# Attention, expert attention and gated FFN in one kernel: six plain pairs instead of two, weight conversions in other places, a first load in two column halves

## The chip, the cores and the metric

The kernel runs on one core of one Trainium2 chip, in one launch. The metric is the device time of an execution in microseconds (us), median of several runs. Before the change it is 498.16 us (three runs, 498.07 to 498.64). PE is the matmul engine, DVE, ACT and POOL are the vector, scalar and GpSimd engines, and SP issues DMAs. Each engine works through its own instructions in order and waits for others by semaphores.

## The reference

Four batches, 448 positions, 12 heads of 64. The output of causal attention is the input of four expert attentions, and theirs that of a gated FFN.

```python
# 1: q, k, v of (4, 12, 448, 64)
scores = scale * q @ k.T;  masked above the diagonal
attn = exp(scores - rowmax);  attn /= sum + 1e-9;  x = attn @ v     # (4, 448, 768)
# 2: four experts of width 64, the two best of x @ w_gate per position
q, k, v = x @ wq[e], x @ wk[e], x @ wv[e]
ye = causal_softmax(scale * q @ k.T) @ v @ wo[e]
out += mask * w * ye
# 3: w_in (768, 1024), w_out (1024, 768), a convolution of 3 along positions
h = relu(x @ w_in)
y = (h * sigmoid(conv3(h))) @ w_out
```

The inputs q, k, v and the expert weights come in float32, the FFN's weights in float64.

## The kernel before

Everything is a task of a small planner (`Program`, with `add` for each task): an engine, an assumed cost, what it needs, and which ring buffer or PSUM bank it takes or frees. Tasks are put out in the order of a table, ORDER, which `steps_of` decodes into pairs of task and engine. It fixes the order of every engine's instructions, and for a task made with `either` also the engine. Where the planner's costs leave PE idle for over 0.7 us, it puts dummy matmuls of an identity (L1563) in between.

Precision is kept by splitting a float32 number into a high part of fewer bits and a low part, its remainder, and by adding products of those parts. The attention works on pairs of heads (A, batch, pair 0 to 5):

- A **split pair** loads q and k of each head twice over the partitions (`nat`, L543), makes high parts (L350, L352 or L356) and two low parts (L359), and multiplies stacked 128 rows in one pass per block (L665). Each head takes one of the three `skA` buffers.
- A **plain pair** loads q and k of both heads once (`load_plain`, L556) into one buffer and multiplies them as plain float32, each head in its half of the 128 rows (`pair_scores`, L622). Before, pairs 0 and 1 of batch 0 are plain.

A head has four blocks of 112 rows, of 112 to 448 columns. Behind the scores come DVE's masked row maxima (L678), ACT's exponentials with their sums (L687), the normalisation on ACT or POOL (L350, L352), transposes on PE (L718), copies out of PSUM (PT), the product with v (L789), and the split of the transposed output xT (L821).

Beside batch 0's attentions the weights are prepared. `fold_piece` multiplies w_in into the experts' wo: twelve pieces of 512 columns, each loaded as float64 (`wraw`, L891), made into float32 by an ACT square (L443) and four DVE steps (L448, L452, L456, L460), split into high (ACT, L898) and low (POOL, L901), and multiplied by 12 matmuls (L910). `proj_weights` loads the experts' q, k, v and gate weights in six slices (`praw`, 512 and 260 columns) and splits them: high on ACT (L954), low on DVE (L958). `wraw` and `praw` share a ring of two buffers. The projections (L981, L1027), the FFN (L1323) and its output products (L1456) follow. The expert pairs of a batch run among the next batch's attentions.

The first load is pair 0 of batch 0: one head on SP's queue, the other on ACT's (L561). SP then loads wo, pair 1 and the first split heads.

Of the kernel before, what the change touches and what calls it, by code (L numbers as in the profile page):

```python
# [17 lines left out]
ALU = mybir.AluOpType  # L18
# [16 lines left out]
    "H>iFzNV?6?qK#-Wfk7A~q%sF_W4I2y1s^2z;Dw}<%(t0WnfIAQJeMFQToFLx3-mmC8T}jacVa(&4ZVdPL<5-<=rqBCcA<CC7D6{+j4+5F#iQ_l"
    "pfAvA^c3L^jRw?20w5$_XHxMN(gFIGASFG+KgTcPm+;f*b^IRw5dVqznYc~bC4E4DPku(G0$jihSO9=XAkGt32~-l5=mM@tO2R1`O@@IqDFh&Z"
    "p16sBPIyh&CL9q?2_oPrFbYfovw)WrA}s*N1cdaQ{F0m?C&^M`2k;0uAX$m{Oj@QC*dYv(`ba-8zY?D_Uow}01Sv@ZC|Bg~vih=yveW>coFaFV"
    "&IoC;i?|9zGZXj|{2BfsX`D0w%#q#!?}15D5;y}cfm_m#WCA5c;!x7SJSj%>5?4s8q}R+-<_(idIb+hu9P%4Lf{|i~EH#G4GGHDOH^^_u5#k=u"
    "OB^On6YrQ-%szRXq9rd<Zpl*eEr7x3$)m(RqJTV0bYX<7pO|l$`^>k@Z!z7NevE)3qYPox6gS00@nRyFG0ZmQn6gV*rc6;Tn6I*=EH(?pQnL&!"
    "8`(#WlZlv4vWt8|IiM_Mtz|6|b!-#c&zizav+S%D)+~#P;b7KScD9@CWCh8+WG`igVxfd7U6h|No0wh9D&>rFh`FSYvM^bnDaV*4VvrT1^pS_i"  # L40
    "d#poNk`>3S5x>dl$mz-Hru>?9l696fKpCXOSskna_6qx!(#z^&4YNjBNz5*Lh&|1oWv{X6S)wdWmLcnL&PvW+&S}mJ<|SqY^N##|)@0UfR*IFv"
    "NV7OuwyaN>8%%&5VLxCW=B(wsXKk|1a^_i=tTanmtE&B#dCS7*pmL}=V2(V;P;0Gq)uwZP&f3XR<-oNM*%}VSIm~*R<I1|oxy7Kd#+=QZIH#Wj"
    "XANWzXOCx3XU}DCXTzKz$H3|2jMeUCFJ`Z0FJ(t-W3`>NqihRjkn=0|gnN{o$Ue<J&%Vq~XZO_h*ACTA<UGrHo)gcV&K=0@%q7=7tG&+#s6;BA"
    "3Q}LxzO3D^U9J^T)l?bvFK#zylRd^U*KO4PTszM`V873q;uxtmDn#{B!_+u+Hutc0o-?1@L7nCFP|vuRTr7CZ?x)`7bmyXThjNqb6nivxggQ#S"
    "WnX38WF6No=l)hJ%(-A&bAGSg;C!mR&w56EP6e{%*_v!(wlSNYovyvB#n!R2h1t|PPMs|q%JyXkvytr8+^yVivp=%|4xJ<7;5jd;uc;f<Evm2%"
    "4=!<ba|yYrTsB9_d7mq*Q`dFYS?a!UF}znfP|iN}EmfS`Q}?9qnEH`=MrDB8oFmSA&M9Z4PLaFAA@MXcBh5yGXg->&4z3H;A$2e7#_FEcQFGb3"
    "np|71K6jY5P8*{w*KO48*L|YCtvku}<py(|xo4ak>OB>p9pql+-sf)7c4&vR_q0hGoD<4Hv$^0LZGpB#`;Prxwvq0mTj@^vb?%G05Isgu(#~j~"
    "X&CyCE+YF2?Gp{;33(6?=1F-(nucfKy|4RN*G2E4579^Iee@~%Ed4cogZ_pd<Xv&DIS8+Vx9YO+5<Gx^#iOx_bSj;|2k8QOl9%Ff_yRti2GY{J"
    "JC2;LqEq=V>3j48dJnIkcgqvdB;ao@1*irS^dubu2f#Q8gF$czoC0NhHUFG`NuL2Hc}~8JHVSrv-Jq8bvW09J+XMn!0{0dFId6mqay48RcL7`m"
# [1578 lines left out]
```

## Time and profile before

| what | value |
|---|---|
| median of three runs | 498.16 us |
| profiled execution, its own time | 498.41 us |
| its span in the trace | 496.6 us |
| PE busy | 477.4 us (96%) |
| DVE, ACT, POOL busy | 414.4, 360.2, 322.7 us |
| DMA | 97.17 MB, mean 196 GB/s |

Times in the profile are of one execution, and the span begins and ends inside the time measured from outside. Matmuls are pipelined, so PE's busy time contains waiting of one for another. The chain of waits is followed back from the last instruction, and the stretches give each engine's busy time in a piece of the span.

### The profile page before, as it was taken

Reading aid. Unit: us, or ns where it says so; the run is one execution under the profiler, and the core shown is the slowest. Engines: PE = TensorE matmul, PEld = TensorE weight load, DVE = VectorE, ACT = ScalarE, POOL = GpSimd, SP = SyncE. Lnnn points to the kernel's source line nnn. Section 1 sums busy time; section 2 is a strip of 40 time slices with the busy share of each in tenths; the row PEclk is TensorE's granted clock in tenths of the full one; section 3 lists DMA queues with packets and bytes.
Section 4 is the critical chain, followed back from the end, with each engine's and each line's share of the span. In section 5 each row is a group of like instructions: output and inputs, shape, how many; then the busy total and the mean of one; then the engine's idle time right before and its main releaser. Section 6 shows DMA issues by size and latency. Waiting matters only on the chain.

```text
span 496.6 us, 10098 instructions
## 1 busy us (share of the span) xinstructions
PE 477.4 (96%) x3142; PEld 405.5 (82%) x3142; DVE 414.4 (83%) x1183; ACT 360.2 (73%) x996; POOL 322.7 (65%) x441
## 2 busy tenths in 40 slices
...
DVE  3999999998899988988889997178898997877852
...
GB/s 183 224 236 239 221 183 181 215 241 228 173 212 238 158 224 203 135 159 261 201 169 209 166 106 232 222 164 196 262 230 229 302 207 252 191 237 130 38 74 94
DMA packets 46534, 97.17 MB, mean 196 GB/s; under 512 B 5136, under 2 KB 26896, under 8 KB 46480
## 3 DMA queue, kind: packets, MB, share of 16 engines
...
HBM read 62.56 MB, written 25.69 MB: 178 GB/s over the span
## 4 chain that ended last, share of the span: by engine, by line
PE 67%; ACT 13%; DVE 9%; POOL 4%; issue 3%; DMA 3%; SPq 0%; POOLq 0%; DVEq 0%; ACTq 0%
PE bank L1456 21%; PE bank L789 10%; PE bank L665 8%; PE bank L981 8%; PE bank L1323 7%; PE bank L718 7%; ACT P_A L687 5%; PE bank L1027 4%; DVE P_A L678 2%; ACT PT_A L350 2%; ACT P_A L350 2%; DMA wraw<-in_w_in_dram 1%; POOL sk_A L359 1%; DMA wset<-wohl 1%; PE bank L1563 1%
## 5 line engine op out<-in xcount | busy, mean ns | idle before, releaser
L687 ACT ACTIVATE P_A<-P_A,nm_A 112x448 f32<-112x448 f32 (+3 forms) x192 | 99.7, 525 | 9.8 <-DVE nm_A L678 8.9
L359 POOL TENSOR_TENSOR sk_A<-nat,sk_A 64x448 fp32r<-64x448 f32 (+1 forms) x76 | 90.4, 1190 | 15.2 <-ACT sk_A L350 7.7
L678 DVE CUSTOM_DVE_ANT_0 P_A<-bank,mask 112x448 f32<-112x448 f32 (+3 forms) x192 | 79.9, 440 | 12.7 <-PE bank L622 6.9
L665 PE MATMUL bank<-sk_A 128*112 128x336 f32 (+3 forms) x352 | 65.0, 310 | 4.8 <-DVE nm_A L678 2.8
L981 PE MATMUL bank<-xT,wqk 128*128 128x448 f32 x288 | 67.8, 372 | 0.0
L718 PE MATMUL bank<-ident,P_A 112*112 112x112 f32 x480 | 59.8, 261 | 5.3 <-ACT PT_A L350 2.9
L665 PEld LDWEIGHTS bank<-sk_A 128*112 128x112 f32 x352 | 48.7, 175 | 13.8 <-DVE nm_A L678 5.7
L718 PEld LDWEIGHTS bank<-ident,P_A 112*112 112x112 f32 x480 | 48.6, 133 | 10.1 <-ACT PT_A L350 3.4
L981 PEld LDWEIGHTS bank<-xT,wqk 128*128 128x128 f32 x288 | 51.5, 188 | 3.7
L350 ACT ACTIVATE P_A<-P_A,r_A 112x336 f32<-112x336 f32 (+3 forms) x101 | 50.6, 530 | 4.6 <-DVE r_A L698 4.6
L352 POOL TENSOR_SCALAR P_A<-P_A,r_A 112x448 f32<-112x448 f32 (+3 forms) x83 | 43.5, 534 | 16.0 <-DVE r_A L698 6.8
L1456 PE MATMUL bank<-up,ws 128*128 128x448 f32 x225 | 52.8, 366 | 0.0
L789 PE MATMUL bank<-PT_A,v 112*64 112x448 f32 (+3 forms) x384 | 49.9, 405 | 1.1 <-DVE PT_A L356 1.1
L1344 DVE SCALAR_TENSOR_TENSOR bank<-h,cw,bank 128x448 f32<-128x448 f32 x64 | 43.1, 685 | 7.7 <-ACT bank L1342 4.7
L350 ACT ACTIVATE PT_A<-bank 112x336 f32<-112x336 f32 (+1 forms) x94 | 42.7, 477 | 4.2 <-PE bank L718 4.1
L789 PEld LDWEIGHTS bank<-PT_A,v 112*64 112x64 f32 x384 | 25.4, 136 | 24.9 <-issue 12.1
L1456 PEld LDWEIGHTS bank<-up,ws 128*128 128x128 f32 x225 | 42.2, 188 | 3.8
L1456 PE MATMUL bank<-us,ws 128*128 128x448 f32 x180 | 43.8, 367 | 0.0
L1027 PE MATMUL bank<-wvg,xT 128*112 128x260 f32 x288 | 42.0, 288 | 0.2 <-DVE lg L1047 0.2
L352 POOL TENSOR_SCALAR P_M<-P_M,r_M,g_w 112x224 f32<-112x224 f32 (+3 forms) x54 | 32.0, 601 | 10.0 <-DVE r_M L698 5.1
L352 POOL TENSOR_SCALAR sk_A<-nat 128x896 fp32r<-128x896 f32 x30 | 28.7, 956 | 14.3 <-DMA nat<-in_qk_dram 13.7
L687 ACT ACTIVATION_READ_ACCUMULATOR P_A<-P_A,nm_A 112x1 f32 x192 | 37.6, 196 | 0.0
...
## 6 DMA issues: line engine op xcount, KB each, us to landing
nat<-in_qk_dram SPq DMA_DIRECT2D x88, 224.0 KB, 4.3
...
g<-g SPq DMA_DIRECT2D x32, 224.0 KB, 2.5
...
v<-in_v_dram SPq DMA_DIRECT2D x24, 224.0 KB, 4.7
out_dram<-osb_c SPq DMA_DIRECT2D x24, 224.0 KB, 2.0
```

The lines of the kernel that those rows point to most:

```text
L350: nc.scalar.activation(dst, src, AF.Copy, scale=scale)
L352: nc.gpsimd.tensor_scalar(dst, src, scale, 1.0 if scale2 is None else scale2, ALU.mult, ALU.mult)
L359: (nc.gpsimd if e == "POOL" else nc.vector).tensor_tensor(dst, a, b, op)
L665: nc.tensor.matmul(sp[:CP], t[:, j.o[h], m * CP : (m + 1) * CP], t[:, j.o[h] + k, :w], start=(k == 2), stop=(k == 1),)
L678: nc.vector.tensor_tensor_reduce(rows(i), st["s", i][:CP, :w], mask[:, S - w :], -SCALE, 3.0e38, ALU.add, ALU.min, st["nm"][:, i : i + 1],)
L687: nc.scalar.activation(rows(i), rows(i), AF.Exp, bias=st["nm"][:, i : i + 1], scale=-1.0, accum_out=st["sm"][:, i, 0:1],)
L718: nc.tensor.transpose(pt[:CP, o : o + CP], rows(i)[:, kt * CP : (kt + 1) * CP], ident[:CP, :CP])
L789: nc.tensor.matmul(st["ov"][h * D : (h + 1) * D, kt * CP : S], j.v[:, kt, h, :], j.PT[h][:, col_base[kt] : col_base[kt] + S - kt * CP], st ...
L981: nc.tensor.matmul(st["ps"][:, :S], proj["wqk"][:, a, cc, w, p * P : (p + 1) * P], xT[b, cc][:, b2, :], start=(cc == 0 and (a, b2) == PASS ...
L1027: nc.tensor.matmul(st[i][:CP, :VW], xT[b, cc][:, a, i * CP : (i + 1) * CP], proj["wvg"][:, b2, cc, :], start=(cc == 0 and (a, b2) == PASSE ...
L1344: nc.vector.scalar_tensor_tensor(y, h, w, y, ALU.mult, ALU.add)
L1456: nc.tensor.matmul(ps(pb)[:, :S], wset[s][:, a, m, c2 * P : (c2 + 1) * P], unit(operands[q, c2, name][0])[:, b2], start=(c2 == 0 and (a, b ...
```

## The change

- All six pairs of batch 0 are plain (`j.p < 6`).
- The first load is cut by columns: both heads' positions 0 to 223 on SP's queue (`load_left`), positions 224 to 447 on ACT's (`load_right`), and the first pair's score blocks go from the narrowest up, the two lower ones needing the left half alone.
- The high parts of the fold's pieces may be made on ACT, DVE or POOL, the low parts on POOL or DVE; the projection weights' high parts on ACT or POOL, their low parts on DVE or POOL; the high parts of the experts' q and k on ACT or DVE.
- Two planner costs change, and the table ORDER is another.

```diff
--- before.py
+++ after.py
@@ -27,75 +27,74 @@
 
 ENGINES = ("ACT", "DVE", "PE", "POOL", "SP", "")
 ORDER = (
-    "c-jTQX-HcMfB@j+CDELkQ<IlObE&!1Txu>..."
...
+    "c-jTQ2}s)uU@-8U=GI(lE;W~$OHKZXF_-4..."
...
 )
 
 
@@ -480,7 +479,7 @@
         order += [A[b, p] for p in range(4)] + [M[b - 1, 0], A[b, 4], A[b, 5], M[b - 1, 1]]
     order += [M[B - 1, p] for p in range(NEP)]
     for j in order:
-        j.plain = j.kind == "A" and j.b == 0 and j.p < 2
+        j.plain = j.kind == "A" and j.b == 0 and j.p < 6
         j.phase = j.b if j.kind == "A" else B + j.b
 
     xT = {}
@@ -556,17 +555,24 @@
         def load_plain():
             alloc_head(j, 0)
             j.qk = f(j.sk[0][:, 0:2, :])
-            if j is order[0]:
-                for h in range(2):
-                    (nc.sync if h else nc.scalar).dma_start(j.qk[h * D : (h + 1) * D], qk[j.b, j.p, h * D : (h + 1) * D])
-            else:
-                nc.sync.dma_start(j.qk, qk[j.b, j.p])
+            nc.sync.dma_start(j.qk, qk[j.b, j.p])
+
+        def load_left():
+            alloc_head(j, 0)
+            j.qk = f(j.sk[0][:, 0:2, :])
+            nc.sync.dma_start(j.qk[:, :, : S // 2], qk[j.b, j.p, :, :, : S // 2])
+
+        def load_right():
+            nc.scalar.dma_start(j.qk[:, :, S // 2 :], qk[j.b, j.p, :, :, S // 2 :])
 
         def load_v():
             j.v = pools["head"].tile([CP, NQ, 2, D], F32, tag="vn", name=f"v_{n}", bufs=RINGS["vn"])
             nc.sync.dma_start(j.v, v[j.b, j.p])
 
-        if j.plain:
+        if j is order[0]:
+            t = add("SP", 700 + dma(224), load_left, take=[j.skb[0]], lag=LAND - 300)
+            j.ready = [t, add("SP", dma(224), load_right, [t], lag=LAND)]
+        elif j.plain:
             t = add("SP", dma(448), load_plain, take=[j.skb[0]], lag=LAND)
             j.ready = [t, t]
         else:
@@ -611,11 +617,13 @@
 
         j.scored = {}
 
+        turns = range(NQ) if j is order[0] else range(NQ - 1, -1, -1)
+
         def score(i):
             def go():
                 w = CP * (i + 1)
                 for h in (1, 0):
-                    if i == NQ - 1:
+                    if i == turns[0]:
                         head_tiles(j, h)
                     j.st[h]["s", i] = sp = ps(j.st[h]["sb", i])
                     r = slice(h * D, (h + 1) * D)
@@ -626,21 +634,21 @@
             return go
 
         first = []
-        for i in range(NQ - 1, -1, -1):
+        for i in turns:
             take = []
             for h in (1, 0):
-                if i == NQ - 1:
+                if i == turns[0]:
                     j.st[h]["Pb"] = Buf("P")
                     take.append(j.st[h]["Pb"])
                 j.st[h]["sb", i] = Buf("s")
                 take.append(j.st[h]["sb", i])
             t = add(
-                "PE", 2 * (CP * (i + 1) / 1.2 + 95), score(i), [j.ready[0]] + first,
+                "PE", 2 * (CP * (i + 1) / 1.2 + 95), score(i), [j.ready[i * 2 // NQ]] + first,
                 take=take, free=[j.skb[0]], mode=2,
             )
             first = [t]
             j.scored[i] = t
-        j.taken = [j.scored[NQ - 1]]
+        j.taken = [j.scored[turns[0]]]
         j.began += j.taken
 
     def head(j, h, moe):
@@ -893,12 +901,12 @@
         t = add("SP", dma(512), load, wo_loads, take=[raw], lag=LAND)
         t, w, buf = from_f64(lambda: st["raw"], raw, t, [P, 2, FW], n)
 
-        def hi():
+        def hi(e):
             st["whl"] = pools["stage"].tile([P, 2, 2, FW], F32R, tag="whl", name=f"whl_{qt}_{c}", bufs=RINGS["whl"])
-            nc.scalar.activation(st["whl"][:, 0], w(), AF.Copy)
-
-        def lo():
-            nc.gpsimd.tensor_tensor(st["whl"][:, 1], w(), f(st["whl"][:, 0]), ALU.subtract)
+            copy(e, st["whl"][:, 0], w())
+
+        def lo(e):
+            two(e, st["whl"][:, 1], w(), f(st["whl"][:, 0]), ALU.subtract)
 
         def prod():
             if c == 0:
@@ -915,9 +923,9 @@
                             stop=(ec == NEP - 1 and cc == NCC - 1 and (a, b2) == PASSES[2]),
                         )
 
-        th = add("ACT", act_sb(n), hi, [t], take=[whl], free=[buf])
-        tl = add("POOL", pool_tt(n), lo, [th], free=[buf])
-        t = add("PE", mm(FW, 4 * NEP * 3 // 2) + 104, prod, [th, tl] + wo_done + last, take=[mb] if c == 0 else [], free=[whl])
+        th = add(either("fhi", 0, of_one(n)), 0, hi, [t], take=[whl], free=[buf])
+        tl = add(either("fol", 0, of_two(n)), 0, lo, [th], free=[buf])
+        t = add("PE", mm(FW, 4 * NEP * 3 // 2) + 30, prod, [th, tl] + wo_done + last, take=[mb] if c == 0 else [], free=[whl])
         fold_tasks.append(t)
         return [t]
 
@@ -949,18 +957,20 @@
                     (proj["wvg"][:, :, cc], r[:, 2 * ED :]),
                 )
 
-            def hi(cc=cc, st=st):
+            def hi(e, cc=cc, st=st):
                 for d, s in parts(cc, st):
-                    nc.scalar.activation(d[:, 0], s, AF.Copy)
-
-            def lo(cc=cc, st=st):
+                    copy(e, d[:, 0], s)
+
+            def lo(e, cc=cc, st=st):
                 for d, s in parts(cc, st):
-                    nc.vector.tensor_tensor(d[:, 1], s, f(d[:, 0]), ALU.subtract)
+                    two(e, d[:, 1], s, f(d[:, 0]), ALU.subtract)
 
             n = 2 * ED + VW
             t = add("SP", dma(386), load, take=[raw], lag=LAND)
-            th = add("ACT", 94 + act_sb(n), hi, [t], free=[raw])
-            tl = add("DVE", 60 + dve(n), lo, [th], free=[raw], port=True)
+            eng = either("phi", 0, {"ACT": 94 + act_sb(n), "POOL": 161 + pool_ts(n)})
+            th = add(eng, 0, hi, [t], free=[raw])
+            eng = either("plo", 0, {"DVE": 60 + dve(n), "POOL": 154 + pool_tt(n)})
+            tl = add(eng, 0, lo, [th], free=[raw])
             w_done[cc] = [th, tl]
 
     def proj_qk(b, p):
@@ -988,10 +998,10 @@
 
                 return go
 
-            def hi(w=w, st=st):
+            def hi(e, w=w, st=st):
                 if w == 0:
                     alloc_sk(j)
-                nc.scalar.activation(j.sk[0][:, 2 * w + 1, :], st["ps"][:, :S], AF.Copy)
+                copy(e, j.sk[0][:, 2 * w + 1, :], st["ps"][:, :S])
 
             def lo(w=w, st=st):
                 nc.vector.tensor_tensor(j.sk[0][:, 2 * w, :], st["ps"][:, :S], f(j.sk[0][:, 2 * w + 1, :]), ALU.subtract)
@@ -1004,7 +1014,8 @@
                 proj_tasks.append(t)
                 last = [t]
             proj_last.setdefault(b, []).append(t)
-            th = add("ACT", act_ps(S), hi, last + ends[:1], take=[skb] if w == 0 else [], free=[mb])
+            eng = either("qkh", 0, {"ACT": act_ps(S), "DVE": dve(S)})
+            th = add(eng, 0, hi, last + ends[:1], take=[skb] if w == 0 else [], free=[mb])
             tl = add("DVE", dve(S), lo, [th], free=[mb])
             ends += [th, tl]
         stack(j, ends)
@@ -1048,7 +1059,7 @@
 
             for cc in range(NCC):
                 t = add(
-                    "PE", mm(VW, 3), part(cc), xdone[b, cc] + w_done[cc] + last,
+                    "PE", mm(VW, 3) + 15, part(cc), xdone[b, cc] + w_done[cc] + last,
                     take=[mb] if cc == 0 else [], free=[xbuf[b, cc]],
                 )
                 proj_tasks.append(t)
```

What the table does at three places follows. In the names, `P_A_1_0` is a probability tile of attention pair 1, head 0 (the batch is not in the name), `nm_A` its maxima, `r_A` its sums; the number at the end counts buffers.

ACT at the program's start, before: `sk_A_0` holds q and k of pair 0, `woT` belongs to the fold.

```order
L393 ACT_TABLE_LOAD
L393 ACTIVATE first_exp<-ltri 112x1
L561 DMA sk_A_0_145<-in_qk_dram 64x896
L851 ACTIVATE woT<-wo_173 128x768
L687 ACTIVATE P_A_0_0_161,sm_90<-P_A_0_0_161,nm_A_0_0_162 112x448
L687 ACTIVATE P_A_0_1_157,sm_88<-P_A_0_1_157,nm_A_0_1_158 112x448
L687 ACTIVATE P_A_0_0_161,sm_90<-P_A_0_0_161,nm_A_0_0_162 112x336
L687 ACTIVATE P_A_0_1_157,sm_88<-P_A_0_1_157,nm_A_0_1_158 112x336
L851 ACTIVATE woT<-wo_192 128x768
```

And now; `wqk` and `wvg` are high parts of the first slice of projection weights, `cwraw` the raw convolution weights.

```order
L392 ACT_TABLE_LOAD
L392 ACTIVATE first_exp<-ltri 112x1
L695 ACTIVATE P_A_0_0_159,sm_90<-P_A_0_0_159,nm_A_0_0_160 112x112
L349 ACTIVATE wqk<-praw_166 128x512
L349 ACTIVATE wvg<-praw_166 128x260
L695 ACTIVATE P_A_0_0_159,sm_90<-P_A_0_0_159,nm_A_0_0_160 112x224
L442 ACTIVATE wm<-cwraw 128x24
L695 ACTIVATE P_A_0_1_155,sm_88<-P_A_0_1_155,nm_A_0_1_156 112x112
L566 DMA sk_A_0_145<-in_qk_dram 128x2x224
L695 ACTIVATE P_A_0_1_155,sm_88<-P_A_0_1_155,nm_A_0_1_156 112x224
L695 ACTIVATE P_A_0_1_155,sm_88<-P_A_0_1_155,nm_A_0_1_156 112x336
L695 ACTIVATE P_A_0_0_159,sm_90<-P_A_0_0_159,nm_A_0_0_160 112x336
```

The issue of half a load has moved from the third row to the ninth, behind conversions of two other loads.

SP's queue at its start, before; `wraw` are raw slices of w_in.

```order
L561 DMA sk_A_0_145<-in_qk_dram 64x896
L846 DMA wo_173<-in_wo_t_dram 128x768
L846 DMA wo_192<-in_wo_t_dram 128x768
L563 DMA sk_A_1_206<-in_qk_dram 128x896
L543 DMA nat_2_1_218<-in_qk_dram 64x896 x2
L1212 DMA cwraw<-in_conv_w_dram 128x24
L891 DMA wraw_0_239<-in_w_in_dram 128x512
L543 DMA nat_2_0_251<-in_qk_dram 64x896 x2
L891 DMA wraw_1_309<-in_w_in_dram 128x512
L543 DMA nat_3_1_335<-in_qk_dram 64x896 x2
```

And now, from its eighth row; `praw` are raw slices of the projection weights.

```order
L558 DMA sk_A_2_293<-in_qk_dram 128x896
L950 DMA praw_305<-in_w_qk_dram 128x512
L951 DMA praw_305<-in_w_vg_dram 128x260
L950 DMA praw_337<-in_w_qk_dram 128x512
L951 DMA praw_337<-in_w_vg_dram 128x260
L570 DMA v_0_378<-in_v_dram 112x512
L950 DMA praw_391<-in_w_qk_dram 128x512
L951 DMA praw_391<-in_w_vg_dram 128x260
L558 DMA sk_A_3_406<-in_qk_dram 128x896
L570 DMA v_2_430<-in_v_dram 112x512
L854 DMA wo_432<-in_wo_t_dram 128x768
L558 DMA sk_A_4_478<-in_qk_dram 128x896
```

The plain pairs' loads have the place of the split heads', and slices of projection weights have the place of w_in's.

DVE in batch 0's second and third pair, before; L448 to L460 are the fold's steps.

```order
L448 TENSOR_SCALAR bank_68<-wraw_0_239 128x512
L678 ISA P_A_1_1_208,nm_A_1_1_209<-bank_65,mask 112x112
L678 ISA nm_A_1_1_209 112x1
L452 SCALAR_TENSOR_TENSOR bank_68<-wraw_0_239,bank_68 128x512
L678 ISA P_A_1_0_212,nm_A_1_0_213<-bank_61,mask 112x112
L678 ISA nm_A_1_0_213 112x1
L456 SCALAR_TENSOR_TENSOR bank_68<-wraw_0_239,bank_68 128x512
L695 TENSOR_REDUCE r_A_1_1_210<-sm_92 112x4
L356 TENSOR_SCALAR PT_A_0_1_1_274<-bank_66 112x336
L698 RECIPROCAL r_A_1_1_210<-r_A_1_1_210 112x4
L460 SCALAR_TENSOR_TENSOR wm<-wm,bank_68 128x512
L678 ISA P_A_2_1_291,nm_A_2_1_292<-bank_62,mask 112x448
```

And now at the same place.

```order
L703 TENSOR_REDUCE r_A_1_1_225<-sm_92 112x4
L706 RECIPROCAL r_A_1_1_225<-r_A_1_1_225 112x4
L686 ISA P_A_2_1_295,nm_A_2_1_296<-bank_62,mask 112x448
L686 ISA nm_A_2_1_296 112x1
L703 TENSOR_REDUCE r_A_1_0_229<-sm_94 112x4
L706 RECIPROCAL r_A_1_0_229<-r_A_1_0_229 112x4
L686 ISA P_A_2_0_299,nm_A_2_0_300<-bank_65,mask 112x448
L686 ISA nm_A_2_0_300 112x1
L686 ISA P_A_2_0_299,nm_A_2_0_300<-bank_62,mask 112x336
L686 ISA nm_A_2_0_300 112x1
L686 ISA P_A_2_1_295,nm_A_2_1_296<-bank_61,mask 112x336
L686 ISA nm_A_2_1_296 112x1
```

The fold's steps are gone from between the maxima, which come from the next pair instead.

## Rows read from the trace of the kernel before

**Rows 1.** The page: busy time, DVE by slices, and the group of softmax exponentials.
```profile
PE 477.4 (96%) x3142; PEld 405.5 (82%) x3142; DVE 414.4 (83%) x1183; ACT 360.2 (73%) x996; POOL 322.7 (65%) x441
...
DVE  3999999998899988988889997178898997877852
...
L687 ACT ACTIVATE P_A<-P_A,nm_A 112x448 f32<-112x448 f32 (+3 forms) x192 | 99.7, 525 | 9.8 <-DVE nm_A L678 8.9
```

**Rows 2.** Stretches: start:end length, busy us (count) by engine, granted PEclk, DMA share, GB/s.
```profile
0.00:12.50 12.50, 11.14 (x52) 8.03 (x52) 4.71 (x20) 6.56 (x17) 2.49 (x13) 1.00 0.67 182
12.50:75.00 62.50, 54.58 (x408) 42.19 (x405) 61.06 (x186) 60.94 (x179) 56.70 (x62) 1.00 0.76 220
75.00:87.50 12.50, 9.00 (x72) 7.66 (x73) 12.50 (x35) 9.93 (x25) 8.69 (x10) 1.00 0.58 178
...
125.00:300.00 175.00, 173.33 (x1304) 142.65 (x1304) 156.35 (x560) 158.57 (x487) 137.82 (x184) 1.00 0.70 187
```

**Rows 3.** The chain that ended last: start us, us, engine tile line, instructions.
```profile
88.74 1.58 PE bank L910 x12
...
125.51 2.04 PE bank L789 x16
...
136.45 0.98 PE bank L718 x10
...
152.17 1.13 PE bank L665 x8
...
325.96 3.60 PE bank L1027 x30
...
432.42 60.66 PE bank L1456 x297
```

**Rows 4.** PE's groups by line from 0 to 87.5 us: shapes, xcount | busy, mean ns.
```profile
L665 PE MATMUL bank<-sk_A 128*112 128x448 f32 (+3 forms) x96 | 18.3, 315 | 4.8 <-DVE nm_A L678 2.8 <-POOL whl L901 1.2 <-DVE sk_A L359 0.4
L910 PE MATMUL bank<-whl,woT 128*128 128x256 f32 x132 | 17.8, 284 | 0.0
L718 PE MATMUL bank<-ident,P_A 112*112 112x112 f32 x130 | 16.7, 264 | 5.2 <-ACT PT_A L350 2.9 <-DVE xT L821 1.2 <-POOL P_A L352 0.7
L789 PE MATMUL bank<-PT_A,v 112*64 112x448 f32 (+3 forms) x86 | 11.8, 414 | 1.1 <-DVE PT_A L356 1.1
...
L622 PE MATMUL bank<-sk_A 64*112 64x448 f32 (+3 forms) x32 | 8.0, 496 | 0.3 <-DVE nm_A L678 0.3
```

**Rows 5.** Groups by line and shape, whole span: xcount | busy us, mean ns of one.
```profile
L359 POOL TENSOR_TENSOR sk_A<-nat,sk_A 128x448 fp32r<-128x448 f32 x37 | 43.1, 1165 | 12.1 <-ACT sk_A L350 7.7 <-PE bank L718 2.6
...
L352 POOL TENSOR_SCALAR sk_A<-nat 128x896 fp32r<-128x896 f32 x30 | 28.7, 956 | 14.3 <-DMA nat<-in_qk_dram 13.7
...
L901 POOL TENSOR_TENSOR whl<-wm,whl 128x512 fp32r<-128x512 f32 x12 | 15.5, 1290 | 2.3 <-PE bank L718 1.6 <-ACT whl L898 0.4
...
L452 DVE SCALAR_TENSOR_TENSOR bank<-wraw,bank 128x512 int32<-128x512 int32 x12 | 8.3, 695 | 0.1
...
L443 ACT ACTIVATE wm<-wraw 128x512 f32<-128x512 f32 x12 | 8.2, 683 | 0.9 <-POOL sk_A L359 0.5 <-DMA wraw<-in_w_in_dram 0.4
...
L958 DVE TENSOR_TENSOR wqk<-praw,wqk 128x512 fp32r<-128x512 f32 x6 | 6.1, 1012 | 0.1
...
L352 POOL TENSOR_SCALAR up<-ux 128x448 fp32r<-128x448 f32 x8 | 4.9, 612 | 2.3 <-PE bank L1456 1.2 <-PE bank L1323 1.0
```

**Rows 6.** Timeline of the start: start us, us, engine, line, operation.
```profile
4.13 0.58 SPq L1212 DMA_DIRECT2D cwraw<-in_conv_w_dram  x1
...
8.27 0.67 ACT L687 ACTIVATE P_A<-P_A,nm_A 112x448 f32<-112x448 f32 x1 [1.51 <-DVE nm_A L678]
...
9.61 0.67 PE L622 MATMUL bank<-sk_A 64*112 64x224 f32 x4
```

**Rows 7.** DMA issues: queue, count, KB each, median us from issue to landing.
```profile
sk_A<-in_qk_dram ACTq DMA_DIRECT2D x1, 224.0 KB, 4.1
...
cwraw<-in_conv_w_dram SPq DMA_DIRECT2D x1, 24.0 KB, 7.1
```

More of the change, by code (lines that the diff above doesn't have):

```diff
@@ L35 @@
[L35 to L49, printed above, removed]
@@ L95 @@
[L95 to L98 removed]
+    "c-jTQ2}s)uU@-8U=GI(lE;W~$OHKZXF_-4l<e$WtQ*)ZczJW&vYTv-vH&EMw+73M4z~c?nc3^A=9vxJDgKFPE?Hj0lgGS##Z9h=k4~%^SwH@sD"
+    "!y~we9s~(VLq-V+LKi`VfFjYzBmx0JLr9Q51Qh`wvWRws2N6WvAT$Ug!iG3SoFkqRCJBRxS;7e71!590hnPbAf?PuGA~{GQ(tzAYcI0&DtRho6"
@@ new lines @@
+    "8RQ9a6|s$2N9-UrkQc}+<Vem~jvVPgYLQ-K8?pl#L~bLeb8eB4oL=Ny&OlBd5|cy95#&g74iO&^d=!B4pn@n1!9nm5(m5+RS=3I>e$EX_gMy;b"
+    "=p?Eg#miylXmad1KN37S;hbcS2}MHpp!!g6b2f91axQaDbL=P%dJr{?8b?i|vN<%g04+m5Bs?Olp<bZoP%Oj{as;`FdQLFpEE4W=ASgOSjW(kl"
+    "=yBvr^aeVEK0&82+o(fS2DO8dpmY!eWE*{fzCxd&eCP<e4LyRnK<%M#(GbiuW)9Pf9zu_x*9eDb45kB}#(<Ck3=u=ea4=eo9HYRRuu1F~W*M`N"
+    "NujqeA2IJS#~1;|fN96>V4%3?NGytkvSUd&JI0L(V-lEOaXnZ%%8MPu{zQ31c|z&L^k9A^yd}IN3}gGSmzXRjj2*{LVP!ZK4vpjB1h{!@8v7bc"
+    "!}%e17%Y~A-NRkrM(|^JR^cl&6l=tRI5#c`nLr=nrqT20ci1)TTkIkB410||$6n#4@wYe#eh#0(9^o+f2<{%P3)hPq!rfxi_+|VVj*e&J*YR)g"
```

115 lines of the change are left out of this document (61 added, 54 removed).

## The prediction

> **What bounds the kernel now.** I read the page's busy lines first, then the stretches, then the chain of waits, and last PE's groups in the first stretch. The page puts PE at 477.4 of 496.6 us and DVE at 414.4, but its digits show DVE at 9 of 10 nearly everywhere between 50 and 100 us and lower later [rows 1]. The stretches say the same with numbers. From 12.5 to 75 us DVE is busy for 61.06 and ACT for 60.94 of 62.5 us, POOL for 56.70 and PE for 54.58. From 75 to 87.5 us DVE is busy all of the 12.50 us and PE only 9.00. From 125 to 300 us it is PE that is full, 173.33 of 175 [rows 2].
>
> PE's busy time also contains waiting, since its matmuls overlap. I therefore price PE's work by dense runs of the chain, where nothing else is waited for [rows 3]: twelve fold matmuls 1.58 us, a pair's sixteen products with V 2.04, ten transposes 0.98, one head's eight split scores 1.13, thirty 260-wide projections 3.60 (120 ns each), 297 products of 448 columns 60.66 (204 ns each). Applied to what PE did before 87.5 us [rows 4]: scores 96/8 x 1.13 = 13.6, fold 132/12 x 1.58 = 17.4, transposes 130 x 0.098 = 12.7, V products 86/16 x 2.04 = 11.0, and two plain pairs at 2.7 (below) = 5.4. That is 60.1 us of PE work in 87.5 us: 27.4 us lost. The whole program (984 matmuls of 448 columns, 288 of 260, 144 of the fold, 640 transposes, 32 pairs of V products, 60 heads of split scores, two plain pairs), priced in the same way, has 455.5 us of PE work in the span of 496.6, so 41.1 us are lost in all, and only 13.7 after 87.5 us. A change that spares vector work before 87.5 us shortens the run; after that, only PE's work counts.
>
> **The change, part by part.** I counted each engine's instructions in the program's order, before and after, up to the place where PE's work reaches 60.1 us, and priced them by the trace's durations. (Before, this count gives DVE 80.2, ACT 79.1 and POOL 69.6 us; the stretches show 78.3, 77.4 and 67.9 busy by 87.5 us [rows 2], so the count is some 2% high.) That place was the V products of batch 0's last pair, with 11 of the 12 fold pieces done. It is now inside the projections of batch 0 (34 of their 448-column and 18 of their 260-wide matmuls done), with no fold product done before it.
>
> DVE falls from 80.2 to 61.0. The fold's steps go from 55 to 15 rows; the big ones take 0.69 each [rows 5], in all -26.2. The projection weights' low parts, ten of 1.01 (the wide) or less, leave for POOL: -7.5. Against that stand score maxima +3.4, probabilities copied out of PSUM (10 to 24) +6.8, transposed x +3.2, and +1.1 of small things.
>
> ACT falls from 79.1 to 65.7. Fold 29 to 6 rows, 0.68 for a square [rows 5]: -12.7. Projection weights' high parts -2.6, splits -1.7, probabilities -3.7, x -2.1. Sixteen more exponentials at 0.52 [rows 1] give +8.3, and the rest +1.0.
>
> POOL falls from 69.6 to 63.2. Splits of q and k go from 35 to 22, at 0.96 (high) and 1.17 (low) each [rows 5]: -14.8. Fold's low parts 12 to 3 at 1.29 [rows 5]: -12.2. Normalisations +4.8. Twenty conversions of projection weights are new there. A low part of 512 columns is like the fold's, 1.29. No row has a 512-wide high part on POOL from SBUF; the nearest are 0.61 for 448 columns and 0.96 for 896 [rows 5], so I take 0.69, bounds 0.61 and 0.96 (on eight of them at most +2 us). In all +15.7.
>
> What is moved out is not gone. Nine more fold pieces stand after that place, among batch 0's projections and batch 1's attentions, where DVE has some slack: from 125 us on it is busy 156.35 of 175, POOL 137.82 [rows 2]. After the place, DVE's total rises by about 4 us, ACT's falls by 2 and POOL's rises by 22. By the count, ACT's load then keeps level with PE's until PE has done 125 us of work, and afterwards every engine stays below PE. I cost this at nothing; if the cover fails, it is case C.
>
> PE gets four more plain pairs. A split pair costs 2 x 1.13 = 2.26 [rows 3]. For a plain pair the one clean row is the 224-column block, both heads: 0.67 [rows 6]. A pair has 1120 columns per head, five such blocks, so at most 3.35, and that row includes the last matmul's drain. I take 2.7, a little under the middle of 2.26 and 3.35. Four pairs: +1.8, between 0 and +4.4.
>
> The Trainium skill speaks against this part: its page "FP8 and Floating Point Precision", section TensorE Precision Notes, says that true FP32 makes four passes through the PE array. With the two heads one after the other that would be 8 passes of 1120 columns at 204/448 ns, 4.08 us a pair, +7.3 for four, and the sum below would be 494.4. The row does not agree if the heads are serial: eight passes of 224 columns would take 0.82 and it took 0.67, so the heads' row halves overlap at least in part.
>
> **The start.** Before, both halves of the first pair were issued at once, and the first exponential began at 8.27 us [rows 6]. Now the right 224 columns are issued from ACT's queue as its ninth row, behind the conversion of cwraw. That transfer was issued at 4.13 us [rows 6] and took 7.1 to land [rows 7]; it is issued earlier now, by my estimate near 2.1, so ACT passes it near 9.2. With the 4.1 us of ACT's former load [rows 7] the right half lands near 13.3. The first pair's two wide blocks wait for it, and everything behind them on PE, the second pair's scores first. Till about 14.5 us ACT then has some 4.1 us of work (table load, four narrow exponentials, one pair of conversions), so it starts 10.4 us late; before, it had lost 12.50 - 6.56 = 5.9 [rows 2]. DVE I put at 12 us late (before, 7.8), by the same wait.
>
> **The sum.** With idle time like that of 12.5 to 75 us (about 2.4% for DVE and ACT [rows 2]), ACT reaches the place at 65.7 + 1.7 + 10.4 = 77.8 us, DVE at 61.0 + 1.5 + 12 = 74.5. Against 87.5 that is 9.7 or 13.0 earlier. PE is fed through both, one after the other, so I take the middle, 11.3. The profiled execution took 498.41 us, 1.8 more than its span and 0.25 over the median of 498.16. So 498.4 - 11.3 + 1.8 = 488.9; I predict 489.
>
> **Rivals.**
> B, larger gain. If the late right half costs nothing in the end (other work is ready for ACT and DVE), their lateness stays at 5.9 and 7.8. The gain is then 14.2 or 17.2, middle 15.7, and the time 484.5. For it speaks that ACT's row for this load stands among conversions it would do anyway; against it, that PE takes its instructions in order.
>
> C, smaller gain. All four engines are now loaded alike (65.7, 63.2, 61.0 and 60.1 in some 76 us), so each slip passes on. At 9% idle instead of 2.4%, ACT loses 4.3 us more, and the same over the next 30 us some 2 to 3 more: 495 to 496, with the middle of the case at 494.5. For it: DVE was full while PE stood in 75 to 87.5 us [rows 2]. Against: with three engines nearly full, 12.5 to 75 us lost DVE only 2.3%.
>
> P, plain pairs at the upper end, +4.4 instead of +1.8 on PE: 491.5. The four-pass rule named above would put it at 494.4. Against both, PE has room in this stage.
>
> E, no change (498): gain and losses cancel, as when the work moved behind the place comes back on PE's path there in full (9 pieces x 4 steps x 0.69 = 25 us of DVE against the 19 spared). Against: DVE's slack after 125 us.
>
> D, slower. SP's queue is in order. The loads of pairs 3, 4 and 5 now stand behind projection-weight loads into a ring of two buffers, and each such load waits until POOL has converted an earlier buffer, which stands behind POOL's normalisations. Before, POOL gated no plain pair's load. If a landing of 4.1 us [rows 7] lies bare at three of the four gates, that is 12.3 us, more than the 9.4 forecast, and the run takes 501.2; two gates give 497.1, so it decides from the third. By my count, pair 3's load lands only just in time (28 to 29 us, wanted at about 29). Against: 14.8 us of splits have left POOL in the same stretch.
>
> **Numbers.** Forecast 0.50 (its own range 486.5 to 492), B 0.17 (480 to 486.5), C 0.16 (492 to 497), P 0.04, E 0.05, D 0.08. The range that holds 8 in 10 runs from 482 to 497: it leaves out the lowest 0.05 of B, E and D, 0.18 in all. This kernel's measurement cannot tell less than 0.2%, about 1 us, so "same" is 497.2 to 499.2. Faster 0.87, same 0.04, slower 0.09.
>
> **What would show it.** In the new profile: the stretch to 75 us with DVE and ACT below what they did before and the fold's steps after it; the 34th of batch 0's projections of q and k on PE (L991) at 75 to 79 us; the right half's landing near 13 us with PE idle before the wide scores; four plain pairs at 2.3 to 3.4 us each; no idle time on PE released by the load of pair 3, 4 or 5. The forecast is wrong if PE waits over 10 us for DVE or ACT between 78 and 125 us, if that projection comes later than 85 us, or if the start costs more than 6 us.

## The result

The changed kernel takes 494.05 us (median of four runs, 492.56 to 494.76) against 498.4 beside it: ratio 0.9909, interval 0.9885 to 0.9934. I had forecast 489. The direction was right; the gain is 4.35 us, less than half of the 9.2 that lie between 498.16 and 489. A second set of twelve runs gave 0.9937 (0.9911 to 0.9963). The profiled execution took 494.76 us with a span of 492.9.

The page's busy line and DVE's slices, as in [rows 1]:

```profile
PE 478.5 (97%) x3148; PEld 404.1 (82%) x3148; DVE 404.7 (82%) x1157; ACT 345.2 (70%) x961; POOL 334.1 (68%) x478
...
DVE  1799988999998889997899896178889988897843
```

DVE lost 10 us of work, and its full slices between 50 and 100 us are no longer all full. The stretches, as in [rows 2] (busy us by engine from PE on: PE, PEld, DVE, ACT, POOL; then granted clock, DMA share, GB/s):

```profile
0.00:12.50 12.50, 9.83 (x41) 7.90 (x42) 1.54 (x14) 4.32 (x13) 6.39 (x18) 1.00 0.66 207
12.50:75.00 62.50, 59.86 (x425) 40.84 (x424) 55.24 (x214) 56.67 (x177) 47.34 (x68) 1.00 0.58 163
75.00:87.50 12.50, 12.47 (x91) 11.39 (x93) 10.93 (x37) 11.89 (x37) 11.90 (x14) 1.00 0.72 209
125.00:300.00 175.00, 171.47 (x1297) 143.75 (x1294) 159.22 (x516) 150.81 (x448) 143.86 (x199) 1.00 0.72 201
```

From 12.5 to 75 us DVE is now busy for 55.24 of 62.5 us and ACT for 56.67, where both had 61. From 75 us on PE is full, which it was only from 87.5 us before. PE's groups up to 87.5 us, as in [rows 4]:

```profile
L726 PE MATMUL bank<-ident,P_A 112*112 112x112 f32 x160 | 20.4, 264 | 0.9 <-POOL P_A L351 0.5 <-POOL wvg L351 0.3
L630 PE MATMUL bank<-sk_A 64*112 64x112 f32 (+3 forms) x96 | 20.0, 456 | 1.3 <-DMA sk_A<-in_qk_dram 1.3
L797 PE MATMUL bank<-PT_A,v 112*64 112x448 f32 (+3 forms) x102 | 13.7, 412 | 0.0
L673 PE MATMUL bank<-sk_A 128*112 128x448 f32 (+3 forms) x64 | 11.1, 307 | 1.8 <-POOL sk_A L358 1.8
...
L991 PE MATMUL bank<-xT,wqk 128*128 128x448 f32 x36 | 9.1, 378 | 0.0
L918 PE MATMUL bank<-whl,woT 128*128 128x256 f32 x36 | 4.7, 285 | 0.0
L1038 PE MATMUL bank<-wvg,xT 128*112 128x260 f32 x18 | 3.1, 297 | 0.0
```

Priced as in the prediction: plain scores 6 pairs x 2.7 = 16.2, transposes 160 x 0.098 = 15.7, V products 102/16 x 2.04 = 13.0, split scores 64/8 x 1.13 = 9.0, projections 36 x 0.204 + 18 x 0.12 = 9.5, fold 36/12 x 1.58 = 4.7. That is 68.1 us of PE work where there were 60.1, so 19.4 us are lost by 87.5 us instead of 27.4: a gain of 8.0. PE's whole work is 457.2 us (455.5 before), so after 87.5 us it loses 492.9 - 457.2 - 19.4 = 16.3 instead of 13.7. The balance: -8.0 + 1.7 + 2.6 = -3.7, the difference of the spans (496.6 and 492.9).

Where the 19.4 us stand, by the same prices: 14.2 of them by 25 us (14.7 before); 2.0 more by 65 us (7.2 before); 2.7 from 65 to 75 us (1.2 before); none from there to 125 us. The two places have a row each. The start, PE's timeline (start us, us, operation; in brackets the idle time before it):

```profile
7.30 2.93 PE L1574 MATMUL bank<-ident 128*128 128x128 f32 x12
11.53 0.82 PE L630 MATMUL bank<-sk_A 64*112 64x336 f32 x4 [1.31 <-DMA sk_A<-in_qk_dram]
```

The wide scores of the first pair begin at 11.53 us, when the right half has landed. And the chain of waits from 57 us on:

```profile
57.05 1.16 POOL sk_A L358
...
58.28 1.15 POOL sk_A L358
...
59.44 0.47 SPq L542
...
59.95 3.90 DMA nat<-in_qk_dram
...
64.03 0.94 POOL sk_A L351
...
65.39 1.12 POOL sk_A L358
...
66.59 1.15 POOL sk_A L358
...
67.78 0.67 PE bank L673 x2
```

A split on POOL ends, only then SP issues the next load of a head of batch 1 (59.44), it lands 3.9 us later, POOL splits it (64.03 to 67.74), and PE's scores have waited for that (67.78). POOL itself stood idle for 3.5 us before the split at 64.03, until the load had landed. PE, DVE and ACT fall short of work in the same stretch, while POOL is busy for 8.90 of 10 us:

```profile
12.50:65.00 52.50, 52.18 (x374) 34.29 (x374) 47.87 (x187) 49.28 (x159) 38.43 (x58) 1.00 0.54 158
65.00:75.00 10.00, 7.68 (x54) 6.54 (x52) 7.38 (x29) 7.39 (x20) 8.90 (x11) 1.00 0.79 187
```

From 12.5 to 65 us PE is busy 52.18 of 52.50; from 65 to 75 us PE, DVE and ACT are all at 7.4 to 7.7 of 10. So the chain has two parts, a transfer and POOL's work behind it.

### The profile page after: what moved, and what is told of

It is laid out like the page before. It is cut to its first block, busy times and chain, and to the rows that moved or that the text cites. A ratio compares the mean times of both kernels' runs of the same rounds, so it can differ in the third digit from the quotient of the medians.

```text
span 492.9 us, 10043 instructions
## 1 busy us (share of the span) xinstructions
PE 478.5 (97%) x3148; PEld 404.1 (82%) x3148; DVE 404.7 (82%) x1157; ACT 345.2 (70%) x961; POOL 334.1 (68%) x478
## 4 chain that ended last, share of the span: by engine, by line
PE 70%; DVE 11%; POOL 8%; ACT 4%; issue 3%; DMA 3%; SPq 0%; POOLq 0%; DVEq 0%; ACTq 0%
PE bank L1467 20%; PE bank L797 9%; PE bank L991 8%; PE bank L726 8%; PE bank L1334 7%; PE bank L673 6%; PE bank L1038 5%; PE bank L918 3%; POOL sk_A L358 3%; DVE P_A L686 2%; PE bank L630 2%; DMA nat<-in_qk_dram 2%; POOL P_A L351 2%; ACT P_A L695 2%; POOL P_M L351 1%
## 5 line engine op out<-in xcount | busy, mean ns | idle before, releaser
L358 POOL TENSOR_TENSOR sk_A<-nat,sk_A 128x448 fp32r<-128x448 f32 (+1 forms) x65 | 75.0, 1154 | 4.7 <-ACT sk_A L349 1.0
L991 PE MATMUL bank<-xT,wqk 128*128 128x448 f32 x288 | 66.1, 371 | 0.0
L726 PE MATMUL bank<-ident,P_A 112*112 112x112 f32 x480 | 61.3, 263 | 3.1 <-DVE xT L829 0.8
L351 POOL TENSOR_SCALAR P_A<-P_A,r_A 112x448 f32<-112x448 f32 (+3 forms) x103 | 52.0, 518 | 14.7 <-ACT P_A L695 7.7
L673 PE MATMUL bank<-sk_A 128*112 128x112 f32 (+3 forms) x288 | 51.4, 306 | 2.5 <-POOL sk_A L358 1.8
L349 ACT ACTIVATE PT_A<-bank 112x336 f32<-112x336 f32 (+1 forms) x97 | 44.0, 478 | 4.4 <-PE bank L726 4.0
L673 PEld LDWEIGHTS bank<-sk_A 128*112 128x112 f32 x288 | 39.9, 175 | 7.1 <-POOL sk_A L358 2.6
L797 PEld LDWEIGHTS bank<-PT_A,v 112*64 112x64 f32 x384 | 25.5, 136 | 23.8 <-issue 11.6
L349 ACT ACTIVATE P_A<-P_A,r_A 112x448 f32<-112x448 f32 (+3 forms) x82 | 40.7, 525 | 2.9 <-DVE r_A L706 2.3
L351 POOL TENSOR_SCALAR P_M<-P_M,r_M,g_w 112x112 f32<-112x112 f32 (+3 forms) x58 | 32.7, 577 | 6.8 <-DVE r_M L706 3.7
L1038 PEld LDWEIGHTS bank<-wvg,xT 128*112 128x112 f32 x288 | 36.2, 175 | 0.9 <-DVE wm L459 0.3
```

The lines of the kernel that those rows point to most:

```text
L349: nc.scalar.activation(dst, src, AF.Copy, scale=scale)
L351: nc.gpsimd.tensor_scalar(dst, src, scale, 1.0 if scale2 is None else scale2, ALU.mult, ALU.mult)
L358: (nc.gpsimd if e == "POOL" else nc.vector).tensor_tensor(dst, a, b, op)
L673: nc.tensor.matmul(sp[:CP], t[:, j.o[h], m * CP : (m + 1) * CP], t[:, j.o[h] + k, :w], start=(k == 2), stop=(k == 1),)
L726: nc.tensor.transpose(pt[:CP, o : o + CP], rows(i)[:, kt * CP : (kt + 1) * CP], ident[:CP, :CP])
L797: nc.tensor.matmul(st["ov"][h * D : (h + 1) * D, kt * CP : S], j.v[:, kt, h, :], j.PT[h][:, col_base[kt] : col_base[kt] + S - kt * CP], st ...
```

## Experiments

Two theories stood against each other. **S**: between 25 and 65 us PE is fed, and what is lost stands at the start (late right half) and at 65 to 75 us (POOL's splits behind their loads). **F**: four engines are full, and the time follows their work. Medians are given with the ratio to the kernel before on the same chip.

**The changed kernel again, as a base.**

> The changed kernel once more, beside the three edits of it, as their base: 493 to 495 us by both theories. Theory S (start and splits): the vector engines no longer set the pace between 25 and 65 us; what is lost stands in the first 25 us (late right half), at 65 to 75 us (POOL's splits for batch 1, each waiting for a load into one of two nat buffers) and in small gaps later. Theory F (four full engines): DVE, ACT and POOL are loaded alike and each slip passes on, so the time follows their total work.

494.76 us, twelve runs from 493.09 to 497.62, ratio 0.9937. The four runs with a mean granted clock of 1.0 took 493.7 us on average, the eight at 0.992 to 0.997 took 495.7. Such a spread is not new: the kernel before ran from 495.12 to 501.49 us beside them, with clocks from 0.992 to 1.0, and there the clock hardly sorted the times (497.6 us on average in the seven runs at 0.998 or more, 498.0 in the others).

**Right half issued at once.**

```diff
         def load_left():
             ...
             nc.sync.dma_start(j.qk[:, :, : S // 2], qk[j.b, j.p, :, :, : S // 2])
+            nc.scalar.dma_start(j.qk[:, :, S // 2 :], qk[j.b, j.p, :, :, S // 2 :])
         def load_right():
-            nc.scalar.dma_start(j.qk[:, :, S // 2 :], qk[j.b, j.p, :, :, S // 2 :])
+            pass
```

> The right half is issued from ACT's queue in the same task as the left half, so it is ACT's third instruction as before the change, and nothing else moves. Both theories: wide scores of the first pair at 6 to 7 us instead of 11.5. Theory S: the 14.2 us lost on PE by 25 us become 10 to 12, and the time falls by 2 to 4 us (490 to 492). Theory F: the work of DVE and ACT is the same, the start is made up for or not by their load: at most 1 us faster (493 to 494.5).

491.93 us, ratio 0.988 (0.9846 to 0.9914), 2.8 us less than the base, as S said; the upper end of the interval just touches the lower end of the base's (0.9911 to 0.9963). All six runs kept the granted clock at 1.0 (491.1 to 493.7). In its profile the wide scores begin at 10.16 us, not at 6 to 7, since twelve dummy matmuls stand before them:

```profile
7.30 2.93 PE L1575 MATMUL bank<-ident 128*128 128x128 f32 x12
10.16 1.00 PE L631 MATMUL bank<-sk_A 64*112 64x336 f32 x4
```

**Low parts of k on DVE instead of POOL.**

```diff
-            return lambda e: two(e, j.sk[h][:, 1, :], ...)
+            return lambda e: two("DVE" if j.b == 1 and j.p < 4 else e, j.sk[h][:, 1, :], ...)
```

> Low parts of k of batch 1's pairs 0 to 3 (8 instructions, 1.17 us each on POOL) are made on DVE (0.73 each) at the same place of the order. Theory S: PE's waits for POOL's splits at 67.8 and 72.3 us (1.8 together) and POOL's wait for the load before them shrink, 1 to 2.5 us faster (491.5 to 493). Theory F: DVE gets 5.8 us more work in a stretch where it is as full as the others: no gain, or up to 2 us slower (494 to 496).

500.18 us, ratio 1.005 (1.0017 to 1.0082), 5.4 us slower than the base: S expected a gain, F at most 2 us of loss. In the trace seven of the eight instructions have moved, since one was on DVE already. Its stretches:

```profile
12.50:40.00 27.50, 27.16 (x174) 15.72 (x173) 22.67 (x95) 24.89 (x80) 18.02 (x32) 0.94 0.56 172
40.00:65.00 25.00, 23.89 (x175) 16.30 (x175) 24.38 (x88) 21.80 (x70) 17.62 (x24) 1.00 0.49 137
65.00:80.00 15.00, 11.18 (x85) 9.78 (x82) 12.49 (x38) 11.12 (x32) 9.02 (x10) 1.00 0.53 144
```

DVE is full from 40 to 65 us (24.38 of 25), and then PE has 11.18 of 15. So the idle 7 us of DVE between 12.5 and 75 us in the changed kernel were no slack: they lie at the start and in the stall after 65 us. In its trace PE waits twice, 3.2 us together, for splits that DVE makes late. The clock of 0.94 before 40 us is a part of the loss too, but not all of it: the three runs with a mean clock of 0.998 or more took 497.8 us on average, the base's four at 1.0 took 493.7. F is right on DVE.

**Projection weights back on ACT and DVE.**

```diff
             def hi(e, cc=cc, st=st):
-                    copy(e, d[:, 0], s)
+                    copy("ACT", d[:, 0], s)
             def lo(e, cc=cc, st=st):
-                    two(e, d[:, 1], s, f(d[:, 0]), ALU.subtract)
+                    two("DVE", d[:, 1], s, f(d[:, 0]), ALU.subtract)
```

> All conversions of the projection weights are put back on ACT (high) and DVE (low) at their places of the new order: POOL loses 15.7 us of work, DVE gets 8 and ACT 3 more before 60 us. Theory F: DVE and ACT are the ones that feed PE, so 3 to 8 us slower (497 to 502). Theory S: both were idle for 9 to 12% between 12.5 and 75 us, and PE is fed: within 2 us of the changed kernel (492.5 to 496).

505.6 us, ratio 1.0147 (1.011 to 1.0184), 10.8 us slower than the base, beyond both expectations. With this one part undone the changed kernel is slower than the one before. The stretch that got the work, and two pieces of it:

```profile
12.50:75.00 62.50, 57.56 (x373) 35.91 (x374) 53.28 (x195) 52.45 (x164) 29.02 (x45) 0.95 0.48 133
```

```profile
20.00:30.00 10.00, 7.69 (x53) 4.98 (x52) 6.41 (x27) 8.93 (x31) 3.52 (x8) 1.00 0.21 66
30.00:40.00 10.00, 9.69 (x58) 5.51 (x57) 8.39 (x33) 8.05 (x25) 4.40 (x8) 0.83 0.57 186
```

DVE and ACT were not fuller: from 12.5 to 75 us they were busy for 53.28 and 52.45 us, less than in the changed kernel (55.24 and 56.67). They waited for each other in order. A low part at the head of DVE's queue waits for ACT's high part (2.40 us until 27.86), the maxima stand behind it, PE then waits 2.31 us for them (until 29.74), and the granted clock is 0.66 from 30 to 35 us. The mean clocks of its runs are 0.985 to 0.993 (base 0.992 to 1.0). Only from 40 us on is DVE full (9.9 of 10 us to 50 us). So the 10.8 us are not simply the price of 11 us of work on full engines; how they divide into order, clock and work is not shown.

**The fold's DVE steps nearly empty.**

```diff
-            nc.vector.tensor_scalar(a, word(1), 3, 0x3FFFFFFF, ...)
+            nc.vector.tensor_scalar(a[:, :, :4], word(1)[:, :, :4], 3, 0x3FFFFFFF, ...)
...
```

> The changed kernel with the fold's four DVE steps cut to 8 of 512 columns (the other columns of w_in are left unconverted): 48 instructions of 0.69 us become about 0.1, some 28 us less work on DVE, of it 20 after 80 us. It prices what I costed at nothing, the fold in its new place. Theory S: the small gaps on PE between 125 and 240 us (5.6 us against 3.0 before) come from that work; they fall by about 2.5, 1.5 to 3 us faster in all. Theory F: DVE is a bound wherever it works; 4 us or more faster. A third view, that the new place is covered as I forecast: under 1 us.

494.57 us, ratio 0.9936 (0.9904 to 0.9968): equal to the base (0.9937), though DVE was busy for 21 us less (382.5 against 403.4 in the base's profile). The two intervals would hide a cost of up to about 2 us. The trace agrees that the fold's DVE steps cost nothing in their new place: from 125 to 300 us PE stands idle for 3.77 us, against 2.92 in the base's profile.

**Zeros for the low part of k.**

```diff
+                nc.gpsimd.memset(f(j.sk[h][:, 1, :]), 0.0)
+                if j.b == 1 and j.p < 4
+                else two(e, j.sk[h][:, 1, :], ...)
```

> The changed kernel with batch 1's pairs 0 to 3 using zeros for the low part of k (8 subtractions of 1.15 us on POOL become fills of about 0.47 on the same engine, 5.4 us less): the repeat of split_on_dve without giving DVE anything. Theory S: PE's waits at 65 to 75 us (3.1 us of loss there) shrink, 1 to 2.5 us faster than the changed kernel. Theory F: POOL is as full as the others, 2 to 4 us faster. If DVE and ACT alone set the pace: under 0.7 us.

492.01 us, ratio 0.9902 (0.9864 to 0.9939), 2.7 us less than the base and 2.6 less than thin_fold on the same chip; the intervals overlap. The waits between 60 and 80 us (us in total, times, longest), of the changed kernel and then of this one:

```profile
POOL sk_A L351 <- DMA nat<-in_qk_dram: 3.5, 1, 3.5
PE bank L673 <- POOL sk_A L358: 1.8, 2, 1.4
```

```profile
POOL sk_A L351 <- DMA nat<-in_qk_dram: 2.2, 2, 1.3
```

PE no longer waits for a split here. So POOL's split chain at 65 to 75 us is a wait of its own. The edit shortens POOL's work and also lets the buffer go earlier (the next load is issued at 56.93 instead of 59.44 us); it does not tell the two apart.

**Zeros for the low parts of the projection weights.**

```diff
             def lo(e, cc=cc, st=st):
-                    two(e, d[:, 1], s, f(d[:, 0]), ALU.subtract)
+                    nc.gpsimd.memset(f(d[:, 1]), 0.0)
```

> The changed kernel with zeros for the low parts of all six slices of projection weights (12 subtractions on POOL of 1.27 and 0.74 us become fills, 6.5 to 7 us less on POOL before 55 us). It prices what the change moved to POOL. Theory F: 2 to 4 us faster than the changed kernel. Theory S, and if DVE and ACT set the pace there: under 0.7 us.

497.34 us, ratio 0.9994 (0.9971 to 1.0017): less work, and 2.6 us more time. PE's timeline and the stretches of its start:

```profile
6.85 1.60 PE L1574 MATMUL bank<-ident 128*128 128x128 f32 x12
13.70 1.47 PE L630 MATMUL bank<-sk_A 64*112 64x336 f32 x4 [5.25 <-DMA sk_A<-in_qk_dram]
```

```profile
10.00:12.50 2.50, 0.00 (x0) 0.00 (x0) 0.00 (x0) 0.00 (x0) 0.00 (x0) 1.00 0.97 316
...
15.00:20.00 5.00, 5.00 (x18) 2.76 (x16) 2.44 (x10) 2.44 (x7) 0.00 (x0) 0.52 0.00 0
20.00:25.00 5.00, 5.00 (x39) 3.32 (x36) 4.31 (x20) 4.63 (x17) 4.16 (x9) 1.00 0.00 0
```

The fills free POOL earlier, so SP issues the next slices of weights earlier (7.89 and 8.90 us instead of 9.60 and 12.47), beside the right half (DMA share 0.97); it lands at 13.7 us, PE stands idle for 5.25 us, and the granted clock is then 0.52 from 15 to 20 us. PE is at 2.4 GHz again after 20 us. The late load is one part of those 5.25 us; the other is that the twelve dummies before it took 1.60 us here and 2.93 in the changed kernel's profile. That alone can be enough: in split_on_dve's profile the right half is there at 11.35 us, no later than in the changed kernel (11.53), but the dummies took 1.60 us, PE stood idle for 2.96, and the clock was 0.50 from 13 to 15 us; after the 1.31 us above it stayed at 1.00. It may be what spreads the base's runs too, but no run of the base with a lowered clock left a trace.

**Both waits taken away together** (right_first and thin_low_k).

> right_first and thin_low_k together (zeros for the low part of k in batch 1's pairs 0 to 3). Theory S, now: my miss is the sum of two waits, the late right half with the fall of the clock behind it (2.8 us in the median) and POOL's split chain at 65 to 75 us (2.7). They lie at different places, so they add: 488.5 to 490, which is the 489 that I forecast. Theory F: the second gain overlaps with the first, 490.5 to 492.

488.82 us, ratio 0.9805 (0.9771 to 0.9839): the two add, 3.1 us under right_first (which ran on another chip, with 0.988). The stretch that stood still is full:

```profile
12.50:65.00 52.50, 52.17 (x374) 34.72 (x372) 48.10 (x186) 50.11 (x161) 39.42 (x62) 1.00 0.62 176
65.00:75.00 10.00, 10.00 (x74) 9.39 (x73) 9.73 (x38) 9.69 (x28) 9.20 (x12) 1.00 0.64 173
```

**Weights' low parts as zeros, right half at once** (right_first and thin_low_w).

> right_first and thin_low_w together (zeros for the low parts of the projection weights, some 7 us less on POOL before 55 us). thin_low_w was 2.6 us slower than the changed kernel, and its trace shows SP's loads issued earlier, the right half landing at 13.7 us instead of 11.5 and the granted clock at its lower level from 13 to 19 us. With the right half out of the way, if that was the reason: equal to right_first or up to 1 us faster (491 to 492.5), so POOL's conversions cost nothing. Theory F: 2 to 4 us faster than right_first (488 to 490). If less work on POOL costs time for another reason: 494 or more.

490.91 us, ratio 0.9849 (0.9822 to 0.9876), 1.0 us less than right_first, inside the noise. With the late half out of the way, 7 us less work on POOL before 55 us are worth about 1 us or nothing, and not the 2 to 4 that F expected. F fails on POOL there.

**No dummies before the wide scores** (right_first, and the planner's second filling left out).

> right_first without the 12 dummy matmuls that the planner put before the first pair's wide scores (7.3 to 10.2 us there); all others stay. The wide scores can follow the narrow ones at 7 to 7.5 us instead of 10.16. If DVE and ACT set the pace from the start on: 1 to 2.5 us faster than right_first (489.5 to 491). If their other waits (pair 1's load, the banks) come in instead: within 0.7 us. If the clock falls for lack of dummies: slower, 493 or more.

490.55 us, ratio 0.9839 (0.981 to 0.9868), all runs from 489.5 to 491.1. It leaves nothing out and beats both kernels: 7.7 us under the one before, 3.5 to 4.2 under the changed one. Against right_first it is 1.4 us less, with intervals that overlap.

**w_out's conversion nearly empty**, on right_no_dummies, edited as thin_fold was.

> right_no_dummies with the four DVE steps of w_out's conversion cut to 8 of 512 columns (the rest of w_out is left unconverted): 48 instructions of 0.69 us, some 28 us less on DVE between 75 and 300 us. After 125 us PE loses 1 to 2.5 us more than before the change until 300 us, and thin_fold has shown that the fold's steps there are not the reason. If DVE's load there is: 488 to 489.5, 1 to 2.5 us faster than right_no_dummies. If DVE is covered there, and the small gaps come from the order or from other engines: within 0.7 us (490 to 491.2).

489.97 us, ratio 0.9854 (0.9821 to 0.9888) against 0.9839: no difference that these runs could show (some 2 us), with 24 us less busy time on DVE. PE's idle time from 125 to 300 us is 3.01 us against 3.53. By the trace DVE is covered after 125 us, but for about half a microsecond at most.

## Why the prediction missed

**The failed step is the gain at the place, 11.3 us, and in it the idle time after the start.** I let ACT arrive at 77.8 us and DVE at 74.5, and took the middle. The place, the 34th projection of q and k, came at about 79.4 us, 8.0 earlier than before. For ACT I had added 65.7 of work, 10.4 at the start and 1.7 of idle time later; the trace shows 65.4, 9.1 (until 13.38 us) and 4.9. For DVE I had 61.0, 12 and 1.5; the trace shows 60.7, 11.0 (until 12.40 us) and 7.8. So the old idle share of 2.4% did not hold, and by luck a start that I had priced too high hid a part of that. Of the idle time, 2.6 us on each of the two stand at 65 to 75 us.

What I had left out is POOL. The sum has no arrival time for it, and I had not followed the splits of batch 1, which are late next once the fold has left. In the profile they wait load by load, and PE with them, for 3 us at 65 to 75 us. POOL had done 57.9 us of work at the place, where I had counted 63.2: it was late, too. (In that count, nine low parts of the fold at 1.29 are 11.6 us, not 12.2.) Removing the wait gives 2.7 us. Taking the middle of the two engines was a second error, argued and not tested: PE's work there needs both, so the later one, ACT, should count (9.7).

That right_thin_k, without that wait and without the late start, takes 488.8 us does not confirm the 489: the forecast had the late start in it.

**What was moved behind the place, at nothing.** For DVE that held: thin_fold and thin_wout gain nothing. Still PE stands idle for 2.6 us more after 87.5 us than before in the profiled execution, 1.9 of them between 125 and 300 us, in gaps of 0.2 to 0.7 us before transposes, scores and products with V. Neither the fold's nor w_out's steps on DVE are the reason; which it is, stays open. With both corrections the sum is 488.9 + 3.2 + 2.6 = 494.7, and 494.76 was measured. That only closes the books, since both corrections are read from the same execution.

**The counts** of ACT and DVE held at the place (65.4 for 65.7, 60.7 for 61.0); POOL's did not (57.9 for 63.2).

**Plain pairs**, estimated at 2.7 us. In dense runs of the chain (start us, us) the four widths, both heads each, take:

```profile
28.84 0.94 PE bank L630 x4
...
37.35 0.75 PE bank L630 x4
...
46.40 0.58 PE bank L630 x4
...
47.82 0.38 PE bank L630 x4
```

Together 2.65 us. P and the four passes one head after the other (4.08) are out. Four passes of both heads side by side would take 4 x 1120 columns at 204/448 ns, 2.04 us, so they overlap for the most part. The Trainium skill, "TensorE: Matmul & The Clock Gate", section Part 3: Packing small matmuls, states that matmuls on different rows of the array run at the same time; the rows agree in kind, not in full.

**The start.** I put the right half's landing at 13.3 us, with ACT 10.4 us late. It was there at 11.53, since cwraw took 3.1 us to land and not 7.1, so that ACT issued the load at 7.85. I had priced the lateness, but not the clock: in two other runs the granted clock fell to 0.50 and 0.52, the lower level of 1.2 GHz, after PE had stood idle for 2.96 and 5.25 us at this place. right_first takes both away, 2.8 us.

**Rivals.** C named about the right time (494.5) and a part of the mechanism: DVE is full between 30 and 65 us (33.9 of 35 us busy), so that work put on it there lengthens the run (split_on_dve). For ACT this is not shown, since praw_back changed order and clock as well, and POOL before 55 us is not full (right_thin_w). C did not name the ring of loads and splits. D did not come: no wait of PE is ended by the load of pairs 1 to 5. B's 484.5 was not reached even with the right half issued at once (right_first). The 34th projection came just outside the 75 to 79 us named for it (79.4), and none of the signs of a wrong forecast appeared: PE waited for 0.3 us between 78 and 125 us, for instance. They were too wide for a miss of 5 us.
